# Two experts' matrix products on one core: another list schedule, from tables of deadline shifts and engine choices, with a look ahead over four products

## The chip, the core and the metric

The kernel runs on one core of a Trainium2 chip. A core has a matrix engine (TensorE, PE in the profile; its weight loads are PEld), a vector engine (VectorE, DVE), an engine for activations (ScalarE, ACT), one for general work (GpSimd, POOL) and one that only issues transfers (SyncE, SP); 16 DMA engines move data between the memory outside (HBM) and the core's own (SBUF). Matrix products are collected in PSUM banks. Each engine works through its own list of instructions in the order in which they were written when the kernel was built, and waits on semaphores for what the others produce. The metric is device time in microseconds (us), the median of several runs; less is better.

## The reference

Attention over 4 batches of 8 heads (576 tokens, 64 columns a head) in which only scores within `tau` of a row's maximum count, and then two experts in a row, each two matrix products with an activation between them:

```python
scores = scale * np.matmul(q, k.transpose(0, 1, 3, 2))
scores = np.where(scores >= np.max(scores, axis=-1, keepdims=True) - tau, scores, -1e9)
attn = softmax(scores); x = np.matmul(attn, v)           # 2304 tokens x 512
h = x @ w1_in                                            # 512 -> 2048
x = (np.maximum(h, 0) + alpha * np.minimum(h, 0)) @ w1_out   # 2048 -> 512
h = x @ w2_in
out = (h / (1 + np.exp(-h))) @ w2_out
```

Everything is float32.

## The kernel before

The attention comes first and takes some 280 us. Its order is written out by hand in `ORDER` and set by another planner, `plan`. The change is in what follows, the two experts.

**How a product is made.** A float32 matrix is split into a rounded part and the rest, so that each product of two matrices is three matmuls: rounded by rounded, rounded by rest, rest by rounded (`TERMS`). A product into one bank is two chunks of 128 rows by three, six matmuls of 128x384 (`product`, L471 to L479). Both matrix products of an expert are done in seven block products instead of eight: sums and differences of blocks are formed first (by DVE or GpSimd) and the results added up afterwards. All but one group of the second products use this scheme (`Seven`, L983); the one that does not is `Plain`.

**The passes.** Each expert is worked in 4 groups of its 2048 inner columns, each group in 3 blocks of 768 tokens: 2 x 4 x 3 = 24 passes (`vi`, L1086). A pass has 14 products from the input into banks A and B (`ab`) and C (`c`), and 14 products back, of the pass before, into banks C and Y (`y`). In a pass:
- The input's pieces `xs` (768 KB each, rounded part and rest) are formed from `X` in the first group of an expert (L456 differences, L465 the rest of the split) and written to HBM (`xd`, L1110); in later groups they are loaded again (L1112). Four buffers turn.
- ScalarE copies banks into `su` (L322, the helper that all copies share), DVE adds these to others (L1131, L1135, L1141), ScalarE takes the activation (L922, L926 for expert 1, L930 for expert 2), DVE ends that of expert 1 (L923, L927). The results are the tiles `r`.
- Sums and differences of `r` (L1003, L1025, for some by a DMA that adds, L1022) are split into `g` (ScalarE rounds, L322; the rest is L1011 or L945), which the products back read.
- DVE adds the products back from banks C and Y to `X` (L975, L976); in the last group these are the result and are stored.
- The next group's weights are loaded (`raw`, L403), decoded (L405 to L410), combined (L418, L424) and split (`w`, L427).

**What sets the order.** All of this is first recorded as a list of 2847 operations, each with an engine, a planned duration and what it depends on. `plan_late` (L202) then walks through planned time. It gives each operation a due time (`late`, counted back from the products in their recorded order, L213 to L224; `OFF` moves whole kinds). Whenever an engine is free it takes, of the operations that can start first, the one due first (L275). TensorE takes its products in the recorded order alone:

```python
c = ([pe[k]] if k < len(pe) and not left[pe[k]] else []) if e == "PE" else cand[e]     # L265
i = min((i for i in c if est(e, i) <= t + 1e-9), key=lambda i: (late[i], i))           # L275
```

Operations marked `BOTH` may run on DVE or GpSimd: they are candidates of both (L231), and GpSimd takes one only where `able` lets it (L248: the due time is far enough, or DVE has enough else to do). The planned times only set the order in each engine's list; the chip keeps that order and waits for real.

Of the kernel before, what the change touches and what calls it, by code (L numbers as in the profile page):

```python
# [56 lines left out]
OFF = {"w": 21.5, "x": 1.8, "t": 2.2, "y": -2.4}  # L57
# [11 lines left out]
POOL_SLACK = 3.28  # L69
# [129 lines left out]
        return [x for x in dict.fromkeys(d) if x != name]  # L199


def plan_late(ops, lead):  # L202

    n = len(ops)
    ops = [(o[0], o[1] * PF, o[2] + o[1] * (PF - 1), *o[3:]) if o[0] in ("DVE", "DVE+", "BOTH") else o for o in ops]
    home = [{"DVE+": "DVE", "BOTH": "DVE", "SWD": "POOL"}.get(o[0], o[0]) for o in ops]  # L210
    after = [[] for _ in range(n)]
    for i, o in enumerate(ops):
        for d in o[3]:  # L213
            after[d].append(i)
    late, t = [1e9] * n, 0.0
    for i, o in enumerate(ops):
        if o[0] == "PE":
            late[i] = t
            t += o[1]
    for i in range(n - 1, -1, -1):  # L220
        o = ops[i]
        for j in after[i]:
            late[i] = min(late[i], late[j] - (o[1] if o[0] == ops[j][0] == "PE" else o[2]))
    late = [x - OFF.get(o[5], 0.0) for x, o in zip(late, ops)]  # L224
    left, ready = [len(o[3]) for o in ops], [0.0] * n
    pe = [i for i, o in enumerate(ops) if o[0] == "PE"]
    free = dict(lead)
    port = {"DVE": 0.0, "POOL": 0.0}
    cand = {e: [] for e in free}

    def enter(i):  # L231
        cand[home[i]].append(i)
        if ops[i][0] == "BOTH":
            cand["POOL"].append(i)

    for i, o in enumerate(ops):
        if o[0] != "PE" and not left[i]:
            enter(i)

    def est(e, i):  # L240
        t = max(free[e], ready[i])
        if e == "DVE" and ops[i][0] != "DVE":
# [17 lines left out]
    k, out = 0, []  # L260
    shift = 0.0
    while True:
        best = None
        for e in free:
            c = ([pe[k]] if k < len(pe) and not left[pe[k]] else []) if e == "PE" else cand[e]  # L265
            if e == "POOL":
                c = [i for i in c if able(i)]
            if c:
                t = min(est(e, i) for i in c)
                if best is None or t < best[0]:  # L270
                    best = (t, e, c)
        if best is None:
            break
        t, e, c = best
        i = min((i for i in c if est(e, i) <= t + 1e-9), key=lambda i: (late[i], i))  # L275
        o = ops[i]
        dur, fin = o[1], o[2]
        if e == "PE":
            k += 1
            shift = max(shift, t - late[i])  # L280
        else:
            cand[e].remove(i)
            if o[0] == "BOTH":
                cand["DVE" if e == "POOL" else "POOL"].remove(i)
# [12 lines left out]
    assert len(out) == n, (len(out), n)  # L297
    return sorted(out, key=lambda x: x[:2]), free
# [3 lines left out]
def attn_moe_moe(  # L302
# [553 lines left out]
    with ExitStack() as pb:  # L856
# [394 lines left out]
```

## Time and profile before

| what | value |
|---|---|
| median of the runs | 1004.07 us (1002.58, 1004.35, 1004.07) |
| profiled execution, first to last instruction | 1002.9 us, 16663 instructions |
| PE busy | 987.9 us (98%), 6044 matmuls |
| PEld busy | 875.2 us (87%) |
| DVE busy | 875.5 us (87%), 1813 instructions |
| ACT busy | 653.0 us (65%) |
| POOL busy | 244.9 us (24%), 170 instructions |
| mean granted clock of TensorE | 0.998 |

The profile is one execution; its own time is its span, 1002.9 us, and 1.2 us lie between this and the median. An engine's busy time is the time in which one of its instructions ran. Neighbouring matmuls overlap, and so do neighbouring instructions of DVE and ACT by some 0.09 us, so that a cost in a row of instructions is read from start to start. In the timeline, the number in brackets is idle time ahead of an instruction, and behind the arrow stands what ended it: engine, tile, line. Buffer numbers are left out there.

### The profile page before, as it was taken

What the parts mean: (1) busy time and instruction counts of PE and PEld (TensorE: products, weight loads), DVE (VectorE), ACT (ScalarE), POOL (GpSimd) and SP (SyncE); (2) the same over time, 40 slices, a digit from 0 to 9 for tenths busy, and PEclk for the clock granted to TensorE, in tenths of its full rate; (3) what the DMA queues carried; (4) which work ended last, traced back from release to release, by engine and by line L of the source; (5) the groups of instructions that cost most, each with busy time, mean ns of one, the idle gap of its engine ahead of it and who ended that gap; (6) DMA issues with size and microseconds to landing.
All of it is one profiled execution on the core that took longest, in us unless ns stands there. A gap on an engine that the chain in (4) does not pass through costs nothing.

```text
span 1002.9 us, 16663 instructions
## 1 busy us (share of the span) xinstructions
PE 987.9 (98%) x6044; PEld 875.2 (87%) x6045; DVE 875.5 (87%) x1813; ACT 653.0 (65%) x1192; POOL 244.9 (24%) x170
## 2 busy tenths in 40 slices
PE   9999999999989999999999999899999999999998
PEld 5666666665679999999999999899999999999997
DVE  7999999999879876899999988899988788878666
ACT  6888889888866665555564556677775565555342
POOL 0000100011033021532432355232223233433111
PEclk9999999999999999999999999999999999999999
DMA  3132222222466685678767676747767667655742
GB/s 115 48 109 84 94 90 81 77 86 67 147 235 242 230 322 194 217 250 288 256 229 243 220 268 214 235 180 263 283 233 263 238 248 245 234 206 195 249 158 105
DMA packets 46051, 194.04 MB, mean 193 GB/s; under 512 B 5392, under 2 KB 8592, under 8 KB 45968
## 3 DMA queue, kind: packets, MB, share of 16 engines
q1 hardware_dynamic: 43936, 187.97, 52.6%
q0 software_dynamic: 1728, 4.72, 2.5%
q8 instruction: 48, 0.79, 0.3%
q10 hardware_dynamic: 304, 0.28, 0.1%
q14 instruction: 35, 0.29, 0.1%
HBM read 150.48 MB, written 37.75 MB: 188 GB/s over the span
## 4 chain that ended last, share of the span: by engine, by line
PE 84%; DVE 8%; issue 3%; ACT 2%; DMA 1%; POOL 0%; ACTq 0%; DVEq 0%; POOLq 0%
PE ab L475 25%; PE c L475 16%; PE y L475 15%; PE s L589 8%; PE t L663 7%; PE pv L697 6%; PE y L959 5%; DVE e L629 1%; DVE x L603 1%; PE t L704 1%; DVE g L1011 1%; PE t L669 1%; DMA xd<-xs 1%; DMA xs<-xd 1%; DVE w L427 1%
## 5 line engine op out<-in xcount | busy, mean ns | idle before, releaser
L475 PE MATMUL ab<-xs,w 128*128 128x384 f32 x1728 | 314.3, 336 | 4.0 <-DVE r L927 2.1
L475 PEld LDWEIGHTS ab<-xs,w 128*128 128x128 f32 x1728 | 300.2, 188 | 7.2 <-ACT cw L405 2.4
L475 PE MATMUL y<-g,w 128*128 128x384 f32 x840 | 157.6, 335 | 1.2 <-DVE X L976 1.2
L475 PEld LDWEIGHTS y<-g,w 128*128 128x128 f32 x840 | 147.1, 188 | 1.7 <-DVE X L976 1.5
L1011 POOL TENSOR_TENSOR g<-r,g 128x768 fp32r<-128x768 f32 x57 | 105.2, 1851 | 174.2 <-ACT g L322 34.7
L322 ACT ACTIVATE g<-r 128x768 fp32r<-128x768 f32 (+1 forms) x143 | 112.0, 795 | 44.7 <-PE c L475 12.7
L603 DVE TENSOR_SCALAR_CACHE_REDUCE x<-s,nsc 128x576 f32<-128x576 f32 x144 | 112.4, 814 | 7.4 <-PE s L589 6.9
L475 PE MATMUL c<-g,w 128*128 128x384 f32 x612 | 115.6, 336 | 1.5 <-DVE g L1011 0.7
L322 ACT ACTIVATE su<-ab 128x384 f32<-128x384 f32 x144 | 70.3, 490 | 69.7 <-PE ab L475 65.1
L475 PEld LDWEIGHTS c<-g,w 128*128 128x128 f32 x612 | 106.6, 188 | 3.6 <-DVE g L1011 1.3
L976 DVE TENSOR_TENSOR X<-y,X 128x384 f32<-128x384 f32 x150 | 82.0, 553 | 29.1 <-PE y L475 28.9
L629 DVE SCALAR_TENSOR_TENSOR e<-x,m,e 128x577 f32<-128x577 f32 x128 | 102.2, 827 | 1.4 <-ACT m L623 1.1
L616 ACT ACTIVATE e<-x,m 128x576 f32<-128x576 f32 x128 | 97.2, 788 | 8.3 <-DVE x L603 8.1
L589 PE MATMUL s<-raw 64*128 64x288 f32 (+1 forms) x576 | 101.0, 428 | 0.7 <-DVE x L603 0.5
L589 PEld LDWEIGHTS s<-raw 64*128 64x128 f32 (+1 forms) x576 | 57.1, 187 | 39.6 <-DVE x L603 12.1
L475 PE MATMUL c<-xs,w 128*128 128x384 f32 x432 | 82.3, 339 | 1.8 <-ACT r L930 1.8
L663 PEld LDWEIGHTS t<-ident,e 128*128 128x128 f32 x576 | 63.2, 141 | 20.5 <-issue 8.9
L663 PE MATMUL t<-ident,e 128*128 128x128 f32 x576 | 79.5, 278 | 0.4 <-DVE e L629 0.4
L322 ACT ACTIVATE pt<-t 128x512 f32<-128x512 f32 x128 | 70.6, 605 | 13.5 <-PE t L663 12.9
L475 PEld LDWEIGHTS c<-xs,w 128*128 128x128 f32 x432 | 76.5, 190 | 2.5 <-ACT r L930 2.1
L427 DVE TENSOR_TENSOR w<-cw,w 128x896 fp32r<-128x896 f32 (+1 forms) x56 | 65.2, 1164 | 8.4 <-ACT w L322 8.3
L322 ACT ACTIVATE w<-cw 128x896 fp32r<-128x896 f32 (+1 forms) x64 | 59.5, 930 | 13.5 <-POOL cw L424 6.5
(100 smaller groups left out, 1423.7 us busy)
## 6 DMA issues: line engine op xcount, KB each, us to landing
xs<-xd SPq DMA_DIRECT2D x126, 768.0 KB, 6.0
xd<-xs SPq DMA_DIRECT2D x42, 768.0 KB, 4.0
raw<-in_w1i SPq DMA_DIRECT2D x16, 512.0 KB, 5.1
raw<-in_w1o SPq DMA_DIRECT2D x16, 512.0 KB, 4.6
raw<-in_w2i SPq DMA_DIRECT2D x16, 512.0 KB, 5.1
raw<-in_w2o SPq DMA_DIRECT2D x16, 512.0 KB, 5.3
rv<-in_v SPq DMA_DIRECT2D x16, 480.0 KB, 3.6
raw<-in_q SPq DMA_DIRECT2D x15, 320.0 KB, 3.3
```

Source lines behind the costliest of these rows:

```text
L322: e.activation(out=dst, in_=src, func=AF.Copy)
L427: st.append(both_step(512 if plain else 896, k + [(key, 0)], [(key, 0)], lambda e: e.tensor_tensor(out=z[:, 1], in0=x, in1=z[:, 0].bitcast ...
L475: T.matmul(bank, WT_[ws[c]][:, x, AI[a], :], xs[:, y, c, :], start=start and k == 0, stop=stop and k == 5, skip_group_check=True,)
L589: T.matmul(SP[u + k][:, hf, :S // 2], RAW[i][p, 0, q], RAW[i][p, 1, c], start=True, stop=True)
L603: V.tensor_scalar(out=x.rearrange("p (a b) -> p a b", a=2), in0=SP[u][:, :, :S // 2], scalar1=nsc, scalar2=None, op0=ALU.mult, op1=ALU.min ...
L616: A.activation(out=ES[u], in_=xts[u % XB][:, 1:S + 1], func=AF.Exp, bias=mcol(u, 0), scale=-1.0)
L629: V.scalar_tensor_tensor(out=e, in0=x, scalar=mcol(u, 1), in1=e, op0=ALU.is_le, op1=ALU.mult, accum_out=mcol(u, 2))
L663: T.transpose(TP[n][:, c * 128:(c + 1) * 128], EP[i, t // 2][:, o:o + 128], ident)
L697: T.matmul(AV[i][h * 64:(h + 1) * 64], RV[i][:, h, kt], src, start=kt == 0, stop=kt == KT - 1)
L959: T.matmul(yt, wview(ws[f])[:, a, i * 128:(i + 1) * 128], half(gs[f, k])[:, c], start=n == 0, stop=n == 3 * G - 1)
L976: V.tensor_tensor(out=dst, in0=src, in1=dst, op=ALU.add))))
L1011: add(*both_step(2 * HN, kr + kg, kg, lambda e: e.tensor_tensor(out=x[:, 1], in0=RP[n], in1=x[:, 0].bitcast(F32), op=ALU.subtract)))
```

## The change

Three things in `plan_late`, all before the chip sees the kernel. (1) Every one of the 2847 operations has a character in `SHIFT` that moves its due time by a multiple of 0.5 us between -16 and +15.5; 676 of them stand for no shift. (2) Every operation has a character in `SIDE`: of the `BOTH` operations 123 are bound to GpSimd (`p`, past the test in `able`) and 213 to DVE (`v`), the others are as before. (3) For TensorE the planner looks at the next four products in the recorded order and takes one of those that can start first, the earliest in that order where several can. The recorded operations and what each computes are the same.

```diff
+LOOK = 4
+DIGITS = "0123456789ABCDEFGHIJKLMNOPQRSTUVWXYZabcdefghijklmnopqrstuvwxyz+-"
+SHIFT = (
+    "7wW00er8HW0WDWzVccEWbsfs7nZInWxM18O0W-Y4eB-0IsWZe0DW1nC0mo-JWRzU-PWlF5uHbyhLMQfa-wqmoi0kounMyAb0VQMz"
...
+SIDE = (
+    "......p.................p..v.......p........v..........v.........v.....v.....vvv.v......pv.v.....vvv"
...
-    late = [x - OFF.get(o[5], 0.0) for x, o in zip(late, ops)]
+    late = [x - OFF.get(o[5], 0.0) + 0.5 * (DIGITS.index(c) - 32) for x, o, c in zip(late, ops, SHIFT, strict=True)]
...
     def enter(i):
-        cand[home[i]].append(i)
-        if ops[i][0] == "BOTH":
-            cand["POOL"].append(i)
+        if ops[i][0] != "BOTH" or SIDE[i] == ".":
+            cand[home[i]].append(i)
+            if ops[i][0] == "BOTH":
+                cand["POOL"].append(i)
+        else:
+            cand["POOL" if SIDE[i] == "p" else "DVE"].append(i)
...
-        if ops[i][0] != "BOTH" or late[i] + shift > max(free["DVE"], ready[i]) + POOL_SLACK:
+        if ops[i][0] != "BOTH" or SIDE[i] == "p" or late[i] + shift > max(free["DVE"], ready[i]) + POOL_SLACK:
             return True
...
-            c = ([pe[k]] if k < len(pe) and not left[pe[k]] else []) if e == "PE" else cand[e]
+            c = [i for i in pe[:LOOK] if not left[i]] if e == "PE" else cand[e]
...
-        i = min((i for i in c if est(e, i) <= t + 1e-9), key=lambda i: (late[i], i))
+        i = min((i for i in c if est(e, i) <= t + 1e-9), key=lambda i: (late[i] if e != "PE" else 0.0, i))
...
         if e == "PE":
-            k += 1
+            pe.remove(i)
```

What this does to the lists is shown at three places, A, C and D; line numbers of the instructions are 69 higher in the new kernel. **A:** DVE in the first two passes. `ab2` and `ab3` are the banks B; the two instructions that write `r5` read them for the last time and so free them. Before, and then now:

```order
L1141 TENSOR_TENSOR ab2_2959<-ab2_2959,su1_3126 128x384
L1141 TENSOR_TENSOR ab3_2960<-ab3_2960,su3_3128 128x384
L410 SCALAR_TENSOR_TENSOR cw_88<-cw_88 128x512
L465 TENSOR_TENSOR xs0_83<-r0_86,xs0_83 128x768
L427 TENSOR_TENSOR w7_3110<-cw_88,w7_3110 128x512
L456 TENSOR_TENSOR r0_86<-X1_74,r0_86 128x768
L927 SCALAR_TENSOR_TENSOR r5_3124<-r5_3124,neg_67,ab2_2959 128x384
L927 SCALAR_TENSOR_TENSOR r5_3124<-r5_3124,neg_67,ab3_2960 128x384
```

```order
L996 SCALAR_TENSOR_TENSOR r4_3123<-r4_3123,neg_67,ab1_2958 128x384
L1210 TENSOR_TENSOR ab3_2960<-ab3_2960,su3_3128 128x384
L534 TENSOR_TENSOR xs0_83<-r0_86,xs0_83 128x768
L996 SCALAR_TENSOR_TENSOR r5_3124<-r5_3124,neg_67,ab3_2960 128x384
L996 SCALAR_TENSOR_TENSOR r5_3124<-r5_3124,neg_67,ab2_2959 128x384
L996 SCALAR_TENSOR_TENSOR r3_3122<-r3_3122,neg_67,su0_3125 128x384
L534 TENSOR_TENSOR xs2_85<-X1_74,xs2_85 128x768
L1014 TENSOR_TENSOR g3_3118<-r5_3124,g3_3118 128x384 x2
```

Four instructions stood between the additions on the banks and the two that free them; one of them is left there. The decoding step of `cw` is ahead of all this now, the split of `w7` is on GpSimd and the difference `r0` comes later; bank 3 is freed ahead of bank 2.

**C:** PE in the seventh pass, where bank `c0` goes over from one product to the next. Before, and then now:

```order
L475 MATMUL c0_3132<-g4_3119,w0_76 128x384 x3
L475 MATMUL c0_3132<-g4_3119,w1_77 128x384 x3
L475 MATMUL c1_3133<-g4_3119,w2_78 128x384 x3
L475 MATMUL c1_3133<-g4_3119,w3_79 128x384 x3
L475 MATMUL y0_3134<-g0_3025,w0_76 128x384 x3
L475 MATMUL y0_3134<-g0_3025,w1_77 128x384 x3
L475 MATMUL y1_3135<-g0_3025,w2_78 128x384 x3
L475 MATMUL y1_3135<-g0_3025,w3_79 128x384 x3
```

```order
L544 MATMUL y0_3134<-g0_3025,w0_76 128x384 x3
L544 MATMUL y0_3134<-g0_3025,w1_77 128x384 x3
L544 MATMUL c0_3132<-g4_3119,w0_76 128x384 x3
L544 MATMUL c0_3132<-g4_3119,w1_77 128x384 x3
L544 MATMUL c1_3133<-g4_3119,w2_78 128x384 x3
L544 MATMUL c1_3133<-g4_3119,w3_79 128x384 x3
L544 MATMUL y1_3135<-g0_3025,w2_78 128x384 x3
L544 MATMUL y1_3135<-g0_3025,w3_79 128x384 x3
```

One product, into `y0`, has moved ahead of the two into the banks C.

**D:** PE where expert 2 begins: products from `xs` with the weights `w8` to `w11` are the new expert's first ones, those with `w4` to `w7` are the products back of expert 1's last pass. Before, and then now:

```order
L475 MATMUL c0_3132<-xs3_3023,w8_3111 128x384 x3
L475 MATMUL c0_3132<-xs3_3023,w9_3112 128x384 x3
L475 MATMUL c1_3133<-xs3_3023,w10_3113 128x384 x3
L475 MATMUL c1_3133<-xs3_3023,w11_3114 128x384 x3
L475 MATMUL c0_3132<-xs4_3024,w4_80 128x384 x3
L475 MATMUL c0_3132<-xs4_3024,w5_81 128x384 x3
L475 MATMUL c1_3133<-xs4_3024,w6_82 128x384 x3
L475 MATMUL c1_3133<-xs4_3024,w7_3110 128x384 x3
L475 MATMUL y0_3134<-g0_3025,w4_80 128x384 x3
L475 MATMUL y0_3134<-g0_3025,w5_81 128x384 x3
L475 MATMUL y1_3135<-g0_3025,w6_82 128x384 x3
L475 MATMUL y1_3135<-g0_3025,w7_3110 128x384 x3
```

```order
L544 MATMUL c0_3132<-xs3_3023,w8_3111 128x384 x3
L544 MATMUL c0_3132<-xs3_3023,w9_3112 128x384 x3
L544 MATMUL y0_3134<-g0_3025,w4_80 128x384 x3
L544 MATMUL y0_3134<-g0_3025,w5_81 128x384 x3
L544 MATMUL c1_3133<-xs3_3023,w10_3113 128x384 x3
L544 MATMUL c1_3133<-xs3_3023,w11_3114 128x384 x3
L544 MATMUL c0_3132<-xs4_3024,w4_80 128x384 x3
L544 MATMUL c0_3132<-xs4_3024,w5_81 128x384 x3
L544 MATMUL y1_3135<-g0_3025,w6_82 128x384 x3
L544 MATMUL y1_3135<-g0_3025,w7_3110 128x384 x3
L544 MATMUL ab0_2957<-xs0_83,w8_3111 128x384 x3
L544 MATMUL ab0_2957<-xs0_83,w9_3112 128x384 x3
```

The first product into `y0` has moved up by three products, the first from the next `xs0` also by three, and the products into the banks C are apart from each other.

DVE at the same place; the last rows are the addition on bank `c0` and the one that empties `y0`. Before, and then now:

```order
L1025 TENSOR_TENSOR r4_3123<-r4_3123,r3_3122 128x768
L424 TENSOR_TENSOR cw_88<-cw_88 128x256
L1011 TENSOR_TENSOR xs4_3024<-r0_86,xs4_3024 128x768
L424 TENSOR_TENSOR cw_88<-cw_88 128x128
L1011 TENSOR_TENSOR g3_3118<-r4_3123,g3_3118 128x768
L1131 TENSOR_TENSOR c0_3132<-c0_3132,su0_3125 128x384
L976 TENSOR_TENSOR X1_74<-y0_3134,X1_74 128x384
L1131 TENSOR_TENSOR c1_3133<-c1_3133,su2_3127 128x384
L976 TENSOR_TENSOR X1_74<-y1_3135,X1_74 128x384
```

```order
L1080 TENSOR_TENSOR g3_3118<-r4_3123,g3_3118 128x768
L477 TENSOR_SCALAR cw_88<-raw0_87 128x512
L475 TENSOR_SCALAR cw_88<-raw0_87 128x512
L1080 TENSOR_TENSOR g2_3117<-r5_3124,g2_3117 128x768
L479 SCALAR_TENSOR_TENSOR cw_88<-cw_88 128x512
L525 TENSOR_TENSOR r1_3120<-X0_73 128x768
L493 TENSOR_TENSOR cw_88<-cw_88 128x128
L525 TENSOR_TENSOR r2_3121<-X0_73,r2_3121 128x768
L493 TENSOR_TENSOR cw_88<-cw_88 128x256
L534 TENSOR_TENSOR xs0_83<-r1_3120,xs0_83 128x768
L1200 TENSOR_TENSOR c0_3132<-c0_3132,su0_3125 128x384
L1045 TENSOR_TENSOR X1_74<-y0_3134,X1_74 128x384
```

Both times the addition that empties `y0` comes right behind the one on `c0`, and fifteen instructions stand between this one and the last subtraction from `X1` ahead of it (more than are shown), six of them of 768 columns before and eight now. The subtraction of bank `c1` from `X1`, which frees `c1`, was ahead of the fifteen and now comes right behind the last row.

## Rows read from the trace of the kernel before

**Rows 1.** Windows: us, busy us per engine (instructions), PEclk, DMA share, GB/s.

```profile
282.20:998.80 716.60, 708.04 (x4046) 702.21 (x4044) 615.31 (x1077) 417.49 (x706) 227.60 (x154) 1.00 0.66 234
715.00:960.00 245.00, 245.00 (x1414) 245.00 (x1413) 203.27 (x342) 138.79 (x229) 77.52 (x53) 1.00 0.66 237
```

**Rows 2.** Timeline, PE: start, us, engine, line, what, count, [idle before <-releaser].

```profile
297.10 2.32 PE L475 MATMUL ab<-xs,w 128*128 128x384 f32 x12 [2.15 <-DVE r L927]
300.33 2.45 PE L475 MATMUL ab<-xs,w 128*128 128x384 f32 x12 [0.90 <-ACT su L322]
399.79 2.32 PE L475 MATMUL ab<-xs,w 128*128 128x384 f32 x12 [0.81 <-DMA xs<-xd]
460.59 2.46 PE L475 MATMUL c<-g,w 128*128 128x384 f32 x12 [0.20 <-DVE r L927]
636.39 3.66 PE L475 MATMUL c<-xs,w 128*128 128x384 f32 x12 [1.76 <-ACT r L930]
650.21 2.37 PE L475 MATMUL y<-g,w 128*128 128x384 f32 x12 [1.20 <-DVE X L976]
986.33 2.18 PE L475 MATMUL c<-g,w 128*128 128x384 f32 x11 [0.55 <-DVE g L1011]
```

**Rows 3.** Windows, columns as in rows 1: the change of experts, its slow matmuls.

```profile
620.00:714.00 94.00, 90.42 (x503) 88.22 (x502) 89.88 (x147) 66.71 (x112) 28.45 (x19) 0.98 0.62 224
637.00:640.30 3.30, 3.30 (x13) 3.30 (x12) 2.01 (x5) 1.22 (x4) 1.71 (x2) 0.51 0.85 148
```

**Rows 4.** Timeline, DVE, first two passes.

```profile
292.90 0.57 DVE L1141 TENSOR_TENSOR ab<-ab,su 128x384 f32<-128x384 f32 x1 [0.35 <-PE ab L475]
293.38 0.71 DVE L410 SCALAR_TENSOR_TENSOR cw<-cw 128x512 int32<-128x512 int32 x1
294.01 0.95 DVE L465 TENSOR_TENSOR xs<-r,xs 128x768 fp32r<-128x768 f32 x1
294.88 0.68 DVE L427 TENSOR_TENSOR w<-cw,w 128x512 fp32r<-128x512 f32 x1
295.48 0.95 DVE L456 TENSOR_TENSOR r<-X,r 128x768 f32<-128x768 f32 x1
296.35 1.13 DVE L927 SCALAR_TENSOR_TENSOR r<-r,neg,ab 128x384 f32<-128x384 f32 x2
```

**Rows 5.** Timeline, ACT, first two passes.

```profile
293.36 0.85 ACT L926 ACTIVATE r<-ab 128x384 f32<-128x384 f32 x2
```

**Rows 6.** Timeline, DVE and ACT, where expert 2 begins.

```profile
623.03 0.55 DVE L975 TENSOR_TENSOR X<-X,c 128x384 f32<-128x384 f32 x1 [0.21 <-PE c L475]
625.41 1.09 DVE L427 TENSOR_TENSOR w<-cw,w 128x896 fp32r<-128x896 f32 x1
633.84 0.57 DVE L1131 TENSOR_TENSOR c<-c,su 128x384 f32<-128x384 f32 x1
634.31 0.56 DVE L976 TENSOR_TENSOR X<-y,X 128x384 f32<-128x384 f32 x1
634.55 1.28 ACT L930 ACT_TABLE_LOAD   x1
635.84 0.49 ACT L930 ACTIVATE r<-c 128x384 f32<-128x384 f32 x1
```

**Rows 7.** A window as in rows 1; the page's issues of tile loads (KB, landing us).

```profile
392.00:402.00 10.00, 9.12 (x52) 8.51 (x51) 8.71 (x14) 6.07 (x11) 4.23 (x5) 1.00 0.92 326
xs<-xd SPq DMA_DIRECT2D x126, 768.0 KB, 6.0
```

**Rows 8.** Lines by form, POOL: busy us, mean ns, idle before.

```profile
L427 POOL TENSOR_TENSOR w<-cw,w 128x896 fp32r<-128x896 f32 x8 | 17.4, 2179 | 166.1 <-ACT w L322 141.0 <-DVE m L638 23.4 <-DVE g L1011 1.6
```

**Rows 9.** Timeline, DVE and POOL at once; the last such DVE instruction.

```profile
297.40 1.82 DVE L465 TENSOR_TENSOR xs<-r,xs 128x768 fp32r<-128x768 f32 x1
296.56 1.84 POOL L465 TENSOR_TENSOR xs<-X,xs 128x768 fp32r<-128x768 f32 x1 [3.02 <-ACT cw L405]
925.15 1.36 DVE L427 TENSOR_TENSOR w<-cw,w 128x896 fp32r<-128x896 f32 x1
```

More of the change, by code (lines that the diff above doesn't have):

```diff
@@ new lines @@
+SIDE = (
+    "......p.................p..v.......p........v..........v.........v.....v.....vvv.v......pv.v.....vvv"
+    ".v......vp.........v.v............v......v.....p..................v......v.......p.......p......p..."
+    "....................p.....v.....v.p.............v.....v..p.........p......p.......v....pv..........."
+    "................v.v.v......pv.........pvp.v.......v..p.............................................."
+    "........................v...v......p......pv.p......p..p.......v.......vp..v........................"
+    "..............p.........................................vv..v.v.vv.p................................"
+    "..........v.........................................vpp.p.p..v.....p......v.p.p......p.v........pv.."
+    "v......ppp.v......................................v.........................................v...v.p."
+    "...v.........p.p.......v.p.........v.......pp......................................................."
+    "............................pvv.p.p...............................................v................."
+    ".........................p....v..v.v...p......v.v.v......vv.........vvv.p......vv..................."
+    "......................p.........................................vvv.v.v.p...v...v......vv.......ppv."
+    "v.....v.p.v.....v.v.p......................................v........................................"
+    ".ppp.v.p.v...v...v......................................p.........................................pp"
+    "..p.v.....p...p......vv.......v.v........v..v.....v.p...v.....v.......v............................."
+    "....................v.............v............v...v..v.vv.........v.v......v........pvv.v.....vvv.."
+    ".p.......p...v........v............v........v.v..................v.............v.p..........v......."
+    ".p....p.......v...p.v......v.....................p.v................................v.v..........vvv"
+    ".v....v..p.....pvp.p.........p......vv.......v.v...........................v........................"
+    "........................pvp.p.......p.....vvp.......v...v.....p.p.v.....v.v.v......................."
+    "..v................................................p.v......pv......................................"
+    "....................................v.v.p.vv...pv.v.....pp..v.....pv..v.....v.........vvv.p........."
+    "...................................................................v.pv.v.p..v......vp.v.....pv....."
+    "...p.p.v......v..p........................................................................v.pvp.vp.v"
+    ".pp..........................................................................v..v..vv....v.......ppv"
+    ".v.....v.v.........v.p.....pv..v.........................v.........................................."
+    "....p.ppv..v.p.v..p................................................................................."
+    "...p....v.vv.p.......................................v........................................p.vvv."
+    "pv.v.pp.v......................................"
+)
@@ L258, in able @@
         return before >= PK * d and other >= PB * d
-    k, out = 0, []
+    out = []
     shift = 0.0
@@ L278, in plan_late @@
         if e == "PE":
-            k += 1
+            pe.remove(i)
             shift = max(shift, t - late[i])
         else:
-            cand[e].remove(i)
-            if o[0] == "BOTH":
-                cand["DVE" if e == "POOL" else "POOL"].remove(i)
+            for q in ("DVE", "POOL") if o[0] == "BOTH" else (e,):
+                if i in cand[q]:
+                    cand[q].remove(i)
         if e == "POOL" and o[0] == "BOTH":
```

29 lines of the change are left out of this document (added).

## Prediction

> **What bounds the kernel now.** I read the page's busy shares first (the table above): TensorE is busy for 98% of the span, so the question is how much of this is waiting after all. The windows answer it. In the experts' part the matmuls follow each other without a gap for long stretches: 245.00 us for 1414 of them is 0.1733 us each, and a product, six of them, is 1.04 us. From the experts' first product to their last, 716.60 us hold 4046 matmuls [rows 1]; at 0.1733 these are 701.2 us. So **15.4 us** is all that another order of the same work can give back. The attention part stands in the same order before and after, no matmul is added or left out, and the additions and stores behind the last product stay too.
>
> Next the timeline of TensorE, for where the 15.4 us lie. A row there starts late, with its releaser in brackets [rows 2]. I count from the start that a matmul would have had, and the first one after a wait takes 0.1 us longer to get going:
> - A, the first two passes: 2.3 us before 297.10 (vector work has not emptied a bank), 1.1 before 300.33; 3.6 us.
> - B, 392 to 400: 1.0 us before 399.79 for a tile that comes by DMA, 0.3 just ahead of it; 1.4 us.
> - C, at 460.59 and in the same way at 548.6: 1.1 us together.
> - D, the change from expert 1 to expert 2 and the two passes behind it, 630 to 708: 1.9 us before 636.39, 1.4 before 650.21, 2.0 in small waits, and 1.9 us because the granted clock is 0.51 from 637.0 to 640.3 [rows 3], the lower level (1.2 GHz), just after TensorE had waited; 7.2 us.
> - E, the last pass: 1.05 us around 986.33 and 0.35 at 964; 1.4 us.
>
> These make 14.7 us; the other 0.7 are single late matmuls.
>
> **The change, part by part.** *The look of four.* It is the planner that may take the first ready of four; the chip still runs one written order. 109 of the 650 products stand elsewhere, three places earlier to eight later. C shows what that is for: in the old order the product into bank c0 came at once and waited for vector work on c0; now a product into y0 stands between. It covers 1.04 us where 0.55 was waited; near 548.6 the product stays in its place, but DVE takes up the work on c0 sooner. C falls from 1.1 to 0.2 us (0 to 1.1, the upper end if y0 is late instead).
>
> *The deadline shifts, at A.* Behind the addition at 292.90 there come, before, a weight step (0.63 from start to start), a split (0.87), a weight split (0.60) and a difference (0.87), and only at 296.35 the two that empty the banks B [rows 4]; the product starts at 297.10. Now only the split is ahead of these two, and the one for bank B1 is first, as B1's product is. From 293.38, 0.87 and 0.60 later it is done, at 294.85, when TensorE comes there at 294.8. ScalarE makes the inputs of the two (from 293.36, 0.4 each [rows 5]); two more of its small activations now stand ahead of them. I take 0.7 us of wait and 0.1 to get going. The 1.1 us before 300.33 go, as the next four products in the old order now come ahead of the one that waited. A falls from 3.6 to 0.8 us (0.3 to 1.5).
>
> *The same, with moved products, at D.* Between the subtraction at 623.03 and the addition on bank c0, DVE now has 15 instructions: eight of 768 columns at 0.87, a weight split at 1.0 (1.09 less the overlap of 0.09), and six weight steps that I put at 2.0, together 10.0 us. With 0.46 for the subtraction itself the addition could start at 633.5; its product lets it start at 633.84 [rows 6]. DVE is just in time. But the addition that frees bank y0 stands behind it and ends at 634.87, and the product into y0, which has been drawn ahead, could start at 633.4: a wait of 1.5 us instead of 1.9. The subtraction that frees c1 now comes after that and ends at 635.3, in time for its product at 635.9. The activation that frees c0 needs a table load of 1.28 us first [rows 6]: 634.4 + 1.28 + 0.5 = 636.2. Its product now comes two places later, at 637.0, so the load is hidden. The waits that followed were for additions and splits that DVE did late; I added up DVE's queue in the same way over the two passes, and behind the 1.5 us nothing in it comes out more than 0.2 us late. D is then 1.7 us, and 1.9 more if the clock falls as before; the wait of 2.3 us before 297.10 did not bring it down (12 matmuls in 2.32 us behind it). I take 2.4 us (1.5 to 4.9).
> The Trainium skill ("ScalarE: Activation LUTs", What ACT_TABLE_LOAD costs) gives a switch of tables 1.28 us and a drain of 1.38. The trace has the 1.28, and the activation starts 10 ns later, so no drain; with one, the product at 637.0 would wait 0.6 us and D be 3.0.
>
> *B, E and the rest.* The tiles that B waits for are issued on SP in the same sequence but for two neighbours, each when TensorE has read its buffer, and in the middle a tile takes 6.0 us to land; from 392 to 402 the DMA engines are busy for 0.92 of the time [rows 7]. Nothing in the change makes that shorter. A weight conversion on ScalarE moves behind an activation that TensorE releases, so that a weight transfer runs later, into this crowd: 1.4 us stay (to 2.5). At E the product that waited 1.05 us has two others ahead of it now, and the wait goes; the 0.35 at 964 is for a tile and stays; and near 907 a product into y1 stands closer behind the addition that frees it, an estimated 0.45: 0.8 us (0.35 to 1.8).
>
> *The engine choices.* 123 instructions are bound to GpSimd and 213 to DVE. By count of the two orders GpSimd has 26 instructions more: 12 more weight splits of 2.18 us [rows 8] and 13 more splits of xs, 19 fewer of g, each 1.84 us or near it [rows 9]; small ones make the rest. GpSimd gets about 21 us more, DVE some 13 less (a split of 768 columns is 0.95 there). What comes is mostly early work, weights of the next group above all; the splits of g, which TensorE reads soon, get the quicker engine. By itself I put this at nothing. But where both run, one waits: the DVE split at 297.40 takes 1.82 us instead of 0.95 while GpSimd runs from 296.56 to 298.40 [rows 9]. There are 37 such DVE instructions, the last at 925.15, which cost 20.3 us in all. In proportion, 21 us more on GpSimd's 227.6 [rows 1] add 1.9 us, most of it where DVE has slack.
> The Trainium skill ("SBUF — State Buffer", Who interferes with whom) says that a DVE instruction with two inputs in SBUF and a GpSimd one that reads it exclude each other, and the later one is blocked fully. The row agrees: 298.40 + 0.82 is the end of that split. This speaks against the change; the third rival is made of it.
>
> *New waits.* Some 40 moved products lie outside A to E, and 26 more slow instructions are about; some will meet an instruction that is late. Below: 0. Above: six collisions of 0.87 with restarts, 6 us. I take 1.2, nearer to nothing, because the passes from 715 to 960 have no wait and DVE idles 42 of 245 us there [rows 1]. Single late matmuls: 0.5.
>
> **The sum.** 0.8 + 1.4 + 0.2 + 2.4 + 0.8 + 0.5 + 1.2 = 7.3 us are left of 15.4, so 8.1 us come off. The profiled execution's span is 1002.9 us and the median of the runs 1004.07; the 1.2 us between them lie outside this. Taken off the median: **996.0 us**. With all lower ends (3.9 us left) it is 992.6, with all upper ends (19) 1008.
>
> **The rivals.**
> 1. *The change of experts keeps its 7.2 us.* DVE is busy for 89.9 of 94 us there [rows 3], the engine choices cancel in these passes (13 instructions each way), and a wait of 1.5 us at the same place may bring the clock down again. Against it: by the sum above the urgent work is now done in time. Then 12.1 us stay: 1000.8 us.
> 2. *Waits of the written order eat the gain.* A product drawn ahead because its inputs were planned to be ready blocks an older one that is ready. For: the planner gives every tile the same time to land. Against: most of the 109 move by one or two places. If one in three loses 0.2 us, 7 us: 1003 us, no difference.
> 3. *Slower: GpSimd blocks DVE just ahead of a product.* At 0.87 us a time [rows 9] nine unhidden ones cancel the gain, and from twelve on the kernel is slower by 0.2%. For: 26 more GpSimd instructions in an order that can't yield. Against: 37 were there before, nearly all hidden, and DVE has idle time in most passes. With 14: 1008 us.
>
> **How the numbers follow.** Under 0.2%, 2 us, a measurement of this kernel can't tell a gain from no change. The forecast has 0.67 (992.5 to 999.5 by itself), rival 1 has 0.14, rival 2 has 0.11, rival 3 has 0.08. Faster: the forecast and most of rival 1, 0.79; the same: 0.13; slower: 0.08. The range leaves out rival 3 and part of rival 2: 992 to 1003.
>
> **What would show it.** From the experts' first product to their last the new trace should lose 8 us with the same count of matmuls. At A the wait on DVE r L927 should be gone and in the last pass that on DVE g; the first late row at D should be a product into y, released by DVE X, after about 1.5 us; B's wait for a tile should still be there; GpSimd should be busy for about 266 us. I am wrong if new waits of 0.5 us and more stand between 410 and 620 or 720 and 960, or if the clock's row at D comes back with waits like the old.

## The result, and the profile after

| | before | after |
|---|---|---|
| median of five runs | 1004.35 us (1002.58 to 1006.60) | 995.45 us (994.49 to 995.88) |
| span of the profiled execution | 1002.9 us | 993.7 us |
| PE busy | 987.9 us (98%) | 984.4 us (99%) |
| DVE busy | 875.5 us, 1813 instructions | 866.8 us, 1787 |
| POOL busy | 244.9 us, 170 instructions | 264.9 us, 196 |

After takes 0.9909 of before's time, with a 95% interval of 0.9896 to 0.9921. A later set of five runs beside other kernels gave 995.04 us and 0.9910 (0.9893 to 0.9927). The forecast was 996.0 us.

The windows of the kernel after, with the columns of [rows 1]: the experts' part, the change of experts, and the passes behind it. The window of the experts' part begins, here as in [rows 1], with the 25th of their matmuls, some 2 us behind the first product that follows the attention (280.02 us before, 280.15 after).

```profile
282.30:990.10 707.80, 704.35 (x4046) 701.24 (x4044) 606.65 (x1051) 416.67 (x708) 247.56 (x180) 1.00 0.68 237
620.00:707.00 87.00, 85.44 (x491) 84.80 (x490) 84.95 (x135) 63.67 (x106) 24.96 (x17) 1.00 0.65 227
707.00:951.00 244.00, 244.00 (x1408) 244.00 (x1407) 201.73 (x340) 137.76 (x230) 84.92 (x58) 1.00 0.68 241
```

The first row answers to the first of [rows 1]: the same 4046 matmuls in 707.80 us instead of 716.60. So 8.8 us of the gain lie there; the start of that matmul is the same to 0.1 us (282.24 before, 282.37 after), and the rest, 0.4 us, lies behind the last product. At 0.1733 us a matmul the part would be 701.2 us; 6.6 us of waits are left of 15.4.

What TensorE waited for in this part, summed by releaser (engine, line, releaser: us in all, times, longest). First the kernel before (its six largest), then the kernel after:

```profile
PE ab L475 <- DVE r L927: 2.1, 1, 2.1
PE c L475 <- ACT r L930: 1.8, 1, 1.8
PE y L475 <- DVE X L976: 1.2, 1, 1.2
PE ab L475 <- ACT su L322: 0.9, 1, 0.9
PE ab L475 <- DMA xs<-xd: 0.8, 1, 0.8
PE c L475 <- DVE g L1011: 0.7, 2, 0.5
```

```profile
PE y L544 <- DVE X L1045: 1.9, 2, 1.2
PE ab L544 <- DMA xs<-xd: 1.0, 2, 0.5
PE y L544 <- ACT X L1041: 0.4, 1, 0.4
PE ab L544 <- ACT su L391: 0.2, 1, 0.2
```

Line numbers are 69 higher after: L1045 is L976 of before, L1041 the copy of a bank to `X` on ScalarE. The waits for `r` and for `g` are gone. The timeline of TensorE has these late rows left; they answer to [rows 2]:

```profile
289.05 0.79 PE L544 MATMUL ab<-xs,w 128*128 128x384 f32 x3 [0.18 <-ACT su L391]
396.58 0.58 PE L544 MATMUL ab<-xs,w 128*128 128x384 f32 x2 [0.48 <-DMA xs<-xd]
528.66 0.97 PE L544 MATMUL y<-g,w 128*128 128x384 f32 x4 [0.69 <-DVE X L1045]
631.35 0.97 PE L544 MATMUL y<-g,w 128*128 128x384 f32 x4 [1.16 <-DVE X L1045]
665.40 0.79 PE L544 MATMUL y<-g,w 128*128 128x384 f32 x3 [0.40 <-ACT X L1041]
956.59 0.93 PE L544 MATMUL ab<-xs,w 128*128 128x384 f32 x4 [0.52 <-DMA xs<-xd]
```

Counted, as in the prediction, from the start that a matmul would have had (the number in brackets, some 0.17 us of start-up, and 0.1 us on the second matmul): 0.46, 0.65, 0.97, 1.43, 0.68 and 0.69 us.

### The profile page after: what moved, and what is told of

Its sections match the earlier page's. It is cut to its first block, busy times and chain, and to the rows that moved or that the text cites. A ratio compares the mean times of both kernels' runs of the same rounds, so it can differ in the third digit from the quotient of the medians.

```text
span 993.7 us, 16656 instructions
## 1 busy us (share of the span) xinstructions
PE 984.4 (99%) x6045; PEld 874.2 (88%) x6045; DVE 866.8 (87%) x1787; ACT 651.2 (66%) x1192; POOL 264.9 (27%) x196
## 5 line engine op out<-in xcount | busy, mean ns | idle before, releaser
L1045 DVE TENSOR_TENSOR X<-y,X 128x384 f32<-128x384 f32 x150 | 82.2, 553 | 22.6 <-PE y L544 22.0
L496 POOL TENSOR_TENSOR w<-cw,w 128x896 fp32r<-128x896 f32 (+1 forms) x21 | 44.2, 2104 | 189.0 <-ACT w L391 156.1
L1080 POOL TENSOR_TENSOR g<-r,g 128x768 fp32r<-128x768 f32 x38 | 70.5, 1855 | 82.2 <-ACT g L391 24.6
L1080 DVE TENSOR_TENSOR g<-r,g 128x768 fp32r<-128x768 f32 x83 | 81.5, 986 | 6.4 <-ACT g L391 6.3
```

Of the source, the lines that this page charges most:

```text
L496: st.append(both_step(512 if plain else 896, k + [(key, 0)], [(key, 0)], lambda e: e.tensor_tensor(out=z[:, 1], in0=x, in1=z[:, 0].bitcast ...
L1045: V.tensor_tensor(out=dst, in0=src, in1=dst, op=ALU.add))))
L1080: add(*both_step(2 * HN, kr + kg, kg, lambda e: e.tensor_tensor(out=x[:, 1], in0=RP[n], in1=x[:, 0].bitcast(F32), op=ALU.subtract)))
```

## The experiments

**Is the gain a sum of parts?** Four kernels take one or two of the three parts away. Each sets constants only; the planner then makes its whole order anew.

```diff
-LOOK = 4                      # no_look
+LOOK = 1
+SHIFT = "W" * len(SHIFT)      # no_shift; look_only (W is a shift of zero)
+SIDE = "." * len(SIDE)        # no_side; look_only
```

No look ahead:

> The tables of shifts and of engine choices as in the kernel after, but TensorE takes its products strictly in program order again (LOOK = 1). Theory 'the parts add up' (the places of the prediction): what the look gave comes back as waits: 0.9 us where the product into c0 waits, 1.1 us just after 300, 0.6 us in the last pass, and about 2.5 us at the change of experts, where a product into y0 and the one behind the table load were moved; so some 5 us more than the kernel after: 1000.5 us. Rival 'one solution as a whole': the tables fit only the order that they were searched with; with another order of the products some 700 of 1787 DVE instructions get another predecessor, and waits of 0.3 to 2 us come up at places that had none: 1003 us or more, the waits then scattered between 410 and 620 and between 710 and 950 us as well.

No shifts:

> The look of four and the table of engine choices as in the kernel after, all deadline shifts zero. 'The parts add up': 2.3 us come back in the first two passes (the vector work that empties the two banks is late again) and about 2.5 at the change of experts: 1000.3 us. 'One solution as a whole': 1003 us or more, with waits at places where neither kernel has one.

No engine bound:

> The look of four and the shifts as in the kernel after, no engine bound by the table (the planner's own rule decides between DVE and GpSimd again). 'The parts add up': the prediction put the engine choices at nothing, so 995.5 us, or 1 to 2 us less because GpSimd then has about 21 fewer instructions that lock DVE out: 994 to 995.5. 'One solution as a whole': some 790 DVE instructions get another predecessor, and it is 3 us or more slower than the kernel after: 998.5 to 1004 us.

The look alone:

> Only the look of four: no shifts, no bound engines. 'The parts add up': of the kernel before's waits go 1.1 us just after 300, 0.9 where c0 is waited for, 0.6 in the last pass: 1001.7 us. 'One solution as a whole': 37 products and 440 DVE instructions stand elsewhere without having been searched for, so gains and losses about cancel: 1003 to 1006 us.

| | median, us | ratio to before (95%) | waits and slow matmuls, experts' part | of these from 600 to 720 |
|---|---|---|---|---|
| before | | | 15.6 us | 7.3 us |
| after | | 0.9909 (0.9896 to 0.9921) | 6.7 | 2.3 |
| no_look | 1030.70 | 1.0275 (1.0256 to 1.0294) | 40.1 | 29.5 |
| no_shift | 1016.53 | 1.0136 (1.0110 to 1.0162) | 30.7 | 18.9 |
| no_side | 1008.56 | 1.0054 (1.0037 to 1.0072) | 18.8 | 14.3 |
| look_only | 1001.84 | 0.9986 (0.9975 to 0.9996) | 13.4 | 9.3 |

The last two columns are taken from the starts of the recorded matmuls, from the 25th on: the time from one to the next, less 0.1733 us, summed. In no_look another 1.5 us of wait lie just ahead of the 25th. With any one part missing, the other two make the kernel slower than before. "The parts add up" is out for these three: it was 30, 16 and 13 us off. It met only the run that has no table at all (1001.7 forecast), and even there the profile shows other waits than forecast: 2.05 us at 664.99 and 1.51 at 698.40 are new. "One solution as a whole" had the direction for these three, and not the place: it expected scattered waits, and over half of them lie around the change of experts in each of the four, where DVE has least room. The longest there, from the timelines of TensorE of no_look, no_shift and no_side:

```profile
637.00 0.69 PE L544 MATMUL ab<-xs,w 128*128 128x384 f32 x1 [5.86 <-DVE xs L534]
```

```profile
662.30 0.69 PE L546 MATMUL y<-g,w 128*128 128x384 f32 x1 [6.74 <-POOL g L1082]
```

```profile
670.41 0.69 PE L546 MATMUL ab<-xs,w 128*128 128x384 f32 x1 [4.52 <-DVE xs L536]
```

Each waits for a single piece of vector work (`xs` or `g`). These runs tell what the change is worth without one of its parts, not how much of the 8.9 us each part gave: a table that fits one order has no price of its own.

**Is it the place of single instructions?** From here on, the order of the kernel after is kept, and a few instructions are moved by hand in the finished list of their engine. Everything else keeps its sequence on every engine.

```diff
 done, ends = plan_late(ops, lead)
+done = put(done, ops, moves)   # takes an instruction out of its engine's list, puts it ahead of
+                               # or behind another, and merges the lists again by what depends on what
```

Three swaps, at the three places where TensorE waited for an engine that could have been earlier. DVE at 528:

```diff
+X1 <- y0, X1
 X1 <- y1, X1
 X1 <- X1, c0
-X1 <- y0, X1
```

DVE at 630, and ScalarE at 664:

```diff
-xs0 <- r1, xs0      (768 columns)
-c0 <- c0, su0
 X1 <- y0, X1
 X1 <- X1, c1
+c0 <- c0, su0
+xs0 <- r1, xs0
```

```diff
+X0 <- y1
 su1 <- ab0
 su3 <- ab1
-X0 <- y1
```

> The kernel after with its written order changed by hand at three places, nothing else: at 528.66, where the product into y0 waits 0.97 us, the addition that frees y0 goes ahead of those that free y1 and c0; at 631.35 (1.43 us) the additions that free y0 and c1 and the one on c0 go ahead of a subtraction of 768 columns that is used 4 us later; at 665.40 (0.68 us) ScalarE's copy that frees y1 goes ahead of two activations on banks A. Theory 'it is the place in the order': all three waits fall under 0.2 us and nothing comes up behind them: 3.1 us less than the kernel after, 992.4 us. Rival 'the engine is full': vector work is busy for 85 of 87 us between 620 and 707, so what one product gains the next ones lose; waits of the same sum turn up within 40 us of each place: 995 to 996 us.

Measured: 994.98 us, 0.9913 of before (0.9901 to 0.9924), which is no measurable difference to after. In the profiles the experts' part is 705.60 us against 707.80 and, in the repeat of after, 706.70. At 528 and 665 no late row is left. At 528 this is as the first theory has it: in the four other runs that keep the order of after there, the repeat among them, the wait was 0.7 to 1.5 us. At 665 it shows nothing: in the repeat of after, with no swap, the product came only 0.25 us late, where it had been 0.68. The third place behaved by the rival. TensorE no longer waits for y0, but it waits twice within 5 us of there, for ScalarE:

```profile
631.30 0.44 PE L560 MATMUL c<-xs,w 128*128 128x384 f32 x1 [0.45 <-ACT r L1015]
635.37 0.45 PE L560 MATMUL c<-xs,w 128*128 128x384 f32 x1 [0.62 <-ACT r L1015]
```

With the start-up these are 1.62 us, where 1.43 were. Two costs that the wait for y0 had hidden came out. Here is ScalarE, DVE and GpSimd of that kernel at the place:

```profile
629.46 1.28 ACT L1015 ACT_TABLE_LOAD   x1 [0.48 <-DVE c L1216]
630.76 0.49 ACT L1015 ACTIVATE r<-c 128x384 f32<-128x384 f32 x1
```

```profile
628.83 0.56 DVE L1216 TENSOR_TENSOR c<-c,su 128x384 f32<-128x384 f32 x1
629.30 1.52 DVE L550 TENSOR_TENSOR xs<-r,xs 128x768 fp32r<-128x768 f32 x1
```

```profile
628.16 1.84 POOL L1096 TENSOR_TENSOR xs<-r,xs 128x768 fp32r<-128x768 f32 x1 [1.64 <-DVE cw L509]
```

The table load starts when the addition on c0 is done (629.39), runs until 630.74, and the product into c0 needs the activation behind it. And the split of 768 columns takes 1.52 us instead of 0.96, as GpSimd works until 630.00.

A second hand version tried to mend that too (the addition on c0 second of the four; the addition on c1 and its activation ahead of a subtraction, a weight split and a conversion; two additions and an activation moved in the first pass).

```diff
 X1 <- y0, X1                 # DVE at 629
+c0 <- c0, su0
 X1 <- X1, c1
-c0 <- c0, su0
 xs0 <- r1, xs0
 ...
+c1 <- c1, su2                # DVE at 632, and its activation r4 <- c1 on ScalarE
 xs1 <- X0, xs1
 w1 <- cw, w1
-c1 <- c1, su2
```

> The kernel after with nine instructions moved by hand. The swaps near 528 and at 665 as in the run with three swaps, which took both waits away. At the change of experts the addition on c0 now comes ahead of the one that frees c1, so that the table load in front of its activation starts 0.3 us sooner, and the addition on c1 and its activation go ahead of a subtraction and a weight split, which made the product into c1 wait 0.90 us there; in the first pass one activation and two additions that empty banks go ahead of work that is used later. Theory 'place in the order': of the 2.9 us of waits in the kernel after at 289, 291 and between 620 and 640, under 1 us is left: the experts' part takes 703.5 to 704 us from first to last product instead of 707.5, and the kernel 3.7 us less than the kernel after: 991.7 us. Rival 'the engine is full': at the change of experts 1.5 us of wait stay, at other instructions than before; 993.5 to 994 us.

Measured: 995.13 us, 0.9914 (0.9896 to 0.9932), again like after, 995.04 on the same chip. The waits at 630 to 636 are down to 0.6 us, and a new one stands at 638.12; in the first pass the waits at 289 and 291 are gone and one of 0.8 us stands at 295.51, where 0.24 were. Near 528, where the same swap had left nothing, two late products stand again: 0.46 us at 527.18 and 0.45 at 531.90.

```profile
295.51 0.45 PE L560 MATMUL ab<-xs,w 128*128 128x384 f32 x1 [0.54 <-DVE r L1012]
638.12 0.44 PE L560 MATMUL c<-g,w 128*128 128x384 f32 x1 [1.12 <-DVE X L1060]
```

Ahead of 638.12 stands a decoding step on DVE that takes 1.34 us instead of 0.46, beside GpSimd; the subtraction behind it frees the bank:

```profile
635.96 1.34 DVE L493 TENSOR_SCALAR cw<-raw 128x512 uint16<-128x512 uint16 x1
637.53 0.54 DVE L1060 TENSOR_TENSOR X<-X,c 128x384 f32<-128x384 f32 x1
```

```profile
635.13 1.85 POOL L550 TENSOR_TENSOR xs<-X,xs 128x768 fp32r<-128x768 f32 x1 [3.40 <-DVE w L512]
```

So at the change of experts what was seen is the rival's: three orders of the same work leave 1.4 to 2 us, each at another instruction. That no order does better is not shown, and "full" is not the whole cause: in both hand versions a DVE instruction at the place is held up beside GpSimd, by 0.56 and 0.88 us, which is what rival 3 of the prediction describes. Neither hand version is shown to beat the kernel after.

The repeat of the kernel after that ran beside it:

> The kernel after itself, unchanged, on the same chip as the two beside it, so that they can be compared with it directly: 995.4 us, 0.991 of the kernel before.

It came out at 995.04 us.

**Was A the place of two instructions, and C the moved product?** The two DVE instructions that empty banks B go back behind two others; the product into y0 at 457 goes back behind those into c0 and c1.

```diff
-r5 <- r5, neg, ab3           # DVE at 295
-r5 <- r5, neg, ab2
 r3 <- r3, neg, su0
 xs2 <- X1, xs2               (768 columns)
+r5 <- r5, neg, ab3
+r5 <- r5, neg, ab2
```

```diff
-y0 <- g0, w0/w1              # PE at 457
 c0 <- g4, w0/w1
 c1 <- g4, w2/w3
+y0 <- g0, w0/w1
```

> The kernel after with two places set back by hand. A: the two instructions that empty the banks B in the first pass go behind one of 384 and one of 768 columns (0.62 and 0.95 us), as far back as in the kernel before. C: the product into y0 goes back behind the two into c0 and c1. Theory of the prediction: the product into B1 waits about 1.6 us longer (its releaser again DVE r), the rest of the pass runs on: 1.6 us more. At C the look covered 0.55 us, so its wait comes back: 0.4 to 0.5. Together 997.5 us. Rival for A, 'given back later': the tile that comes by DMA at 396.58 keeps its time, the wait for it falls from 0.75 to 0: 0.8 us more in all. Rival for C, 'the vector work did it': DVE ends its work on c0 at 457.04 where the product would now come at 457.02: no wait comes back.

Measured: 999.99 us, 0.9964 (0.9952 to 0.9975). The wait at A is back with its old releaser, but it is 2.7 us, where 1.6 more than the 0.24 of after had been expected; below it DVE's list, which shows why, and the granted clock behind it.

```profile
300.68 0.66 PE L560 MATMUL ab<-xs,w 128*128 128x384 f32 x1 [2.52 <-DVE r L1012]
```

```profile
297.46 0.61 DVE L1012 SCALAR_TENSOR_TENSOR r<-r,neg,su 128x384 f32<-128x384 f32 x1
299.05 0.96 DVE L550 TENSOR_TENSOR xs<-X,xs 128x768 fp32r<-128x768 f32 x1 [0.98 <-ACT xs L407]
299.93 1.13 DVE L1012 SCALAR_TENSOR_TENSOR r<-r,neg,ab 128x384 f32<-128x384 f32 x2
```

```profile
300.60:303.80 3.20, 3.12 (x10) 3.15 (x11) 3.14 (x6) 2.03 (x5) 0.00 (x0) 0.54 0.93 292
```

I had counted the durations of the two instructions that were put in front, 1.57 us. The second of them waits 0.98 us for ScalarE, and all that stands behind it on DVE waits with it. Then the clock is 0.54 for ten matmuls, most of them at 0.32 us, 1.4 us more. At C the rival is right: in the old order of products only 0.2 us of delay is there (463.75). So it is DVE's earlier work on c0, not the moved product, that took C's wait away. The tile at 397 was not given back either: 0.6 us there, as in after. The longer wait, the clock and the 0.2 us make 4.0 of the 4.5 us by which this run is longer than after; the rest is not accounted for here.

**Does the clock follow the wait?**

```diff
-X1 <- y0, X1                 # DVE at 630.7
 X1 <- X1, c1
 X1 <- y1, X1
 cw <- cw
+X1 <- y0, X1
```

> The kernel after, but at the change of experts the addition that frees y0 goes three instructions further back, so that the product that waits 1.43 us at 631.35 waits some 1.3 us longer. Theory 'the clock follows the length of the wait': with 2.7 us of wait TensorE's granted clock falls to its lower level (about 0.5) for a dozen matmuls, as it did in the kernel before after 1.92 us: 1.3 + 1.9 = 3.2 us more than the kernel after, 998.6 us. Rival 'it does not': the clock stays at 1.0 as it did at 297 of the kernel before after 2.3 us: 1.3 us more, 996.8 us.

Measured: 999.29 us, 0.9957 (0.9943 to 0.9971); the wait, and the window behind it:

```profile
633.81 0.69 PE L560 MATMUL y<-g,w 128*128 128x384 f32 x1 [2.74 <-DVE X L1061]
```

```profile
633.80:639.90 6.10, 6.09 (x19) 6.09 (x20) 3.26 (x4) 3.16 (x5) 1.41 (x2) 0.50 0.71 205
```

The clock falls to its lower level, for 19 matmuls. In these traces it fell as well after waits of 1.92 us (before, 636.39 [rows 2, 3]), 2.05 (look_only, 664.99) and 2.68 (the run above), and after one of 1.51 that another of 0.7 followed 0.9 us later (look_only, 698.40). It stayed at 1.00 after 1.43 (after, 631.35) and 1.71 (no_look, 649.35), but also after 2.31 (before, 297.10 [rows 2]), 2.00 (no_look, 301.06) and 2.57 (old_sides, 489.97). The first row is after, the others are old_sides:

```profile
631.35:634.50 3.15, 3.15 (x18) 3.15 (x19) 3.15 (x6) 3.14 (x5) 1.81 (x2) 1.00 0.73 253
```

```profile
489.97 0.44 PE L577 MATMUL ab<-xs,w 128*128 128x384 f32 x1 [2.40 <-ACT su L424]
489.90:494.00 4.10, 4.03 (x23) 4.03 (x24) 4.00 (x7) 3.31 (x7) 0.87 (x1) 1.00 0.56 173
```

So the wait's length alone does not decide it; what else does stays open.

**Is the choice of engine worth nothing?** The order of after, with the engines of before: first for all 186 instructions that differ, then for the 56 of them between 707 and 951 us.

```diff
+done = put([(*x[:3], "DVE" if x[2] in TO_DVE else "POOL" if x[2] in TO_POOL else x[3]) for x in done], ops, [])
```

> The written order of the kernel after, but the 186 instructions that have another engine there than in the kernel before go back to their old engine (106 from GpSimd to DVE, 80 from DVE to GpSimd), each at its place in the order. Theory of the prediction, 'the choice of engine by itself is worth nothing': 994 to 997 us. Rival 'order and engines belong together': the 80 that TensorE reads soon take 1.85 us on GpSimd instead of 0.95, and the 106 push urgent vector work back by up to 1 us each; waits of 0.3 us and more at over ten places: 1001 us or more.

> The written order of the kernel after, with the old engines again only for the 56 instructions between 707 and 951 us (31 go from GpSimd to DVE, 25 from DVE to GpSimd), where DVE is idle for 42 of 244 us and no product waits. Theory of the prediction, 'the choice of engine by itself is worth nothing where there is room': no wait comes up, 995 to 996 us. Rival 'order and engines belong together': with all 186 set back four waits came up in this stretch (2.95, 0.47, 0.71 and 0.91 us, and a fall of the clock), so 4 to 7 us more: 1000 to 1002 us.

Measured: 1043.60 us, 1.0400 (1.0386 to 1.0413), for all; 998.18 us, 0.9940 (0.9927 to 0.9954), for the 56, 3.1 us more than after on the same chip. The four late rows of the second, where after has none between 707 and 951:

```profile
722.65 0.44 PE L570 MATMUL c<-g,w 128*128 128x384 f32 x1 [0.24 <-ACT r L1025]
811.99 0.44 PE L570 MATMUL c<-g,w 128*128 128x384 f32 x1 [0.55 <-ACT r L1025]
833.24 0.44 PE L570 MATMUL ab<-xs,w 128*128 128x384 f32 x1 [0.15 <-ACT r L1025]
876.95 0.45 PE L570 MATMUL c<-g,w 128*128 128x384 f32 x1 [0.74 <-DVE X L1071]
```

With start-up they are 2.8 of the 3.1 us. The prediction's view is refuted in both runs: with this order the engines are not free to choose, even where DVE idles 42 of 244 us. The rival had the direction; its 4 to 7 us for the second run were too many, since neither the wait of 2.95 us nor the fall of the clock came back.

## Why the prediction was right

The sum came out at 6.7 us left where 7.3 were forecast. In part this is luck: B came out 0.75 us lower and the single late matmuls 0.7 higher, which cancel, and in the repeat of after 5.5 us are left. The ends of the range were added up slightly wrong: the lower terms make 4.1 us, not 3.9, and the upper ones 18.3, not 19. Term by term:

| term | forecast, us | measured |
|---|---|---|
| A, first two passes | 0.8 (0.3 to 1.5) | 0.94: 0.46 at 289.05, 0.24 each at 291.37 and 295.77 |
| B, the tile at 397 | 1.4 | 0.65 (0.38 in the repeat) |
| C | 0.2 | 0 |
| D, change of experts | 2.4 (1.5 to 4.9) | 2.1: 1.43 at 631.35, 0.68 at 665.40 (1.44 and 0.25 in the repeat) |
| E, last pass | 0.8 (0.35 to 1.8) | 0.69, a tile (0.33 in the repeat) |
| new waits | 1.2 (0 to 6) | 1.14: 0.97 at 528.66, 0.17 at 572.66 |
| single late matmuls | 0.5 | 1.2 |

- **A** was right in place and cause. DVE's list there, which answers to [rows 4]: behind the addition (293.76) only the split is left ahead of the two.

```profile
293.76 0.57 DVE L1210 TENSOR_TENSOR ab<-ab,su 128x384 f32<-128x384 f32 x1
294.24 0.95 DVE L534 TENSOR_TENSOR xs<-r,xs 128x768 fp32r<-128x768 f32 x1
295.11 1.14 DVE L996 SCALAR_TENSOR_TENSOR r<-r,neg,ab 128x384 f32<-128x384 f32 x2
```

  The first of them ends at 295.71, and the product into B1 starts at 295.77, 0.24 us late, where 0.8 had been put down. About half of what is left at A, the 0.46 us at 289.05, is another instruction, ScalarE's copy of a bank A. The run that sets the two back shows that their place holds 2.7 us, and the clock besides.
- **D** was right in its main row: the first late product is one into y0, released by DVE `X`, after 1.43 us where 1.5 were worked out, and the clock stays at 1.00 behind it. The table load [rows 6] is hidden, as forecast:

```profile
630.27 0.56 DVE L1200 TENSOR_TENSOR c<-c,su 128x384 f32<-128x384 f32 x1
630.91 1.28 ACT L999 ACT_TABLE_LOAD   x1 [0.43 <-DVE c L1200]
632.21 0.49 ACT L999 ACTIVATE r<-c 128x384 f32<-128x384 f32 x1
```

  Its product starts at 633.57, when the one ahead of it is done. The activation follows the load by 20 ns, so the second price, that of the Trainium skill's drain ("ScalarE: Activation LUTs", What ACT_TABLE_LOAD costs), is again not there. The run with three swaps shows the other side: where the load was not covered, the product waited.
  The wait at 665.40 was not foreseen: it is for ScalarE, whose queue I had not added up. But most of it is the chance of one execution. ScalarE itself had waited there for a transfer to HBM that frees a buffer of `xs`, 1.45 us in after and 1.02 in the repeat, where the product came 0.25 us late; first after, then the repeat:

```profile
662.81 0.85 ACT L391 ACTIVATE xs<-X 128x768 fp32r<-128x768 f32 x1 [1.45 <-DMA xd<-xs]
```

```profile
662.43 0.85 ACT L391 ACTIVATE xs<-X 128x768 fp32r<-128x768 f32 x1 [1.02 <-DMA xd<-xs]
```

- **C** fell as forecast, but for the second of the two reasons that the prediction gave for the two places; the moved product at 460 covers next to nothing.
- **B** was forecast to stay at 1.4 and fell to 0.65. No order on SP explains it: with the same order around it the tile was waited for 0.38, 0.65 and, in the run with the later y0, 1.39 us. The term is the chance of one execution, and the forecast had taken one draw for its size.
- **E**: the wait for `g` is gone, as forecast; the estimated 0.45 us near 907 did not come, and the tile's wait was 0.69 instead of 0.35.
- **New waits** had the right size and by the text's own test the wrong place: it said that a wait of 0.5 us or more between 410 and 620 would show it wrong, and 528.66 is one. That test was stricter than the sum, which held 1.2 us for such. The run with three swaps shows its cause: DVE frees y1 and c0 first, and TensorE asks for y0 first. The product stands where it stood before; it is the order on DVE that the shifts changed. Rival 2's mechanism, a product drawn ahead that waits, is seen at 665.40 (two places earlier than before) and 631.35 (three), not elsewhere.
- **The engine choices**: GpSimd is busy for 264.9 us where 266 were forecast. The price of nothing held for what the added GpSimd work costs. Counting DVE instructions of the experts' part that take over 0.2 us and over a quarter longer than the median of their line and shape, DVE's lengthening rose from 19.1 us (33 instructions) to 23.4 (25), more than the forecast's 1.9, and none of them comes just ahead of a late product above. The longest, with the GpSimd row that overlaps it (as in [rows 9]):

```profile
920.92 2.58 DVE L1072 TENSOR_TENSOR r<-r,r 128x768 f32<-128x768 f32 x1 [2.02 <-POOL g L1080]
```

```profile
919.04 3.64 POOL L1080 TENSOR_TENSOR g<-r,g 128x768 fp32r<-128x768 f32 x2 [1.14 <-ACT g L391]
```

  What was wrong is the sentence beside it, that the choices are worth nothing by themselves: set back, they cost 3 us where DVE has room and 48 us in all. They belong to the order that they were chosen with.

Rival 1 (the change of experts keeps 7.2 us) and rival 3 (GpSimd blocks DVE ahead of a product) did not happen. What rival 3 describes does happen in the kernels with a part missing: in no_side, ahead of the wait at 670.41, a weight split of DVE at 660.61 takes 2.50 us instead of 1.09, with GpSimd at work until 662.16, and a step of 0.68 at 665.52 takes 1.69, with GpSimd at work until 666.66. It also stands ahead of late products in the two hand versions.

## What to carry to other kernels

When only the order changes, forecast the places where the busiest engine waits today, one by one, and add up the queue of each engine that feeds them, ScalarE's too; the bound is what those places hold (15.4 us here, 1.5% of the time). An instruction put ahead of another on an in-order engine costs its own wait besides its duration. The parts of such a schedule can't be priced one by one: with one of three missing it was worse than the old schedule. And a wait of under a microsecond is read from a repeat too, before a cause is given to it: 0.68 us at 665.40 were 0.25 in the next profile of the same kernel.

## What the runs showed of the hardware

- A table load on ScalarE doesn't run ahead of its activation's wait: in after and in the run with three swaps it starts 0.08 and 0.07 us behind the end of the DVE instruction that the activation needs, with ScalarE idle for 0.43 and 0.48 us before it. So a ScalarE that is free early did not hide it; products placed between did.
- The wait for one DMA tile, in the same order, varied from 0.38 to 1.39 us between executions, and with the same order up to there the first product behind the attention started at 279.8 to 282.5 us. Differences of 1 to 2 us between single profiles of this kernel mean nothing by themselves: the hand versions, 0.4 to 2.2 us shorter in the experts' part than the two profiles of after, can't be told from it by their medians.
- All kept traces together have 20 waits of 1.5 to 3 us in the experts' part. After 11 of them (1.51 to 2.95 us) the granted clock fell to its lower level, after 9 (1.54 to 2.57 us) it did not; in the run that sets two places back and the one with the later y0 the fall cost 1.4 us (10 matmuls) and 2.9 us (19).
